# Linear attention and two expert layers in one kernel: the state's scaling on ScalarE, one mask operation for two score halves, weight splits and the last routing batch moved

## The chip, the cores and the metric

The kernel runs on 1 core of a Trainium2 chip. The metric is device time in microseconds. Engines: TensorE (PE; PEld is its weight load), VectorE (DVE), ScalarE (ACT), GpSimd (POOL) and SyncE (SP), which issues most transfers. A line number is that of the kernel before, unless the text says otherwise.

## What is computed

```python
for t in range(S):                       # attention, per batch and head; D = 48, S = 768
    state = alpha[:, :, t, :, None] * state + np.einsum('bhd,bhe->bhde', k[:, :, t], v[:, :, t])
    y[:, :, t] = np.einsum('bhd,bhde->bhe', q[:, :, t], state)
...
logits = xn @ en.T / tau                 # rows of x and of the 8 experts' embeddings, normalized
expert_idx = np.argmax(logits, axis=1)   # each of 3072 tokens goes to one expert
...
    out[mask] = gate_w[mask, None] * (np.maximum(x[mask] @ w1[e], 0.0) @ w2[e])
...
h = np.maximum(np.maximum(x @ w1, x @ w2), x @ w3)   # last layer, for all tokens
return (h @ w_out).astype(np.float32)
```

## The kernel before

The 3072 tokens are 24 groups of 128: 4 sequences of 6. Eight heads are four pairs, and a pair's two heads lie on partitions 0 to 47 and 64 to 111. In a group the recurrence is done by products: VectorE makes the decay's running products from both sides (`undo`, L274, and `decay`, L287, two scans of 516 columns), keys and queries are weighed by them (L294 on VectorE, L289 on GpSimd), and the state that passes from group to group (`sbar`) is the sum of the group's own product and the state before (L382), scaled per row and pair by the next group's decay (L384).

Attention is software-pipelined in one written order, which is also the order on each engine's queue. Iteration g of the loop issues on TensorE: `sv(g)` (masked scores times values, tile xT, L339), `kback(g+1)` (keys transposed, kb, L329), `scores(g+1)` (sc, L314), `by_token(g-1)` (output turned to tokens, with the experts' logits, xp, L357), `qs(g)` (queries times state, added to xT, L347) and `update(g)` (st, L378). The first group of a sequence has no qs product, the last no kback and no update. On VectorE stand: the scans of group g+2, the mask of g+1 (`causal`, L321, one operation for each half of the pairs, each half in a bank of PSUM), keys of g+2, logits of g-1 (L365), L382 and L384. ScalarE copies kb, xp and xT out of PSUM, squares xp (jx) and runs a range check over both running products (jk, L298). GpSimd weighs queries and scatters tokens' rows to their expert's place in memory (L469).

Routing runs in batches of groups (`SIZES`); a batch's steps on VectorE, with one ranking product on TensorE (rk, L407 to L410), are spread over the iterations by `slot("P")` to `slot("E")` and a string of letters. `fetch_first` reads the first 224 rows of the first expert back (xa) once 18 groups are scattered.

Weights of the experts come in units of 128 hidden columns. A unit is split into two float32r parts by `split_w(u)`: two casts on ScalarE (L218, L219), then, a step later, one subtraction on GpSimd (L221) and one on VectorE (L222). Units 0 to 4 are split during the last iterations, cast behind iteration 19 + u and subtracted behind sv of the next.

After the loop: `turn_first` (three pairs of transposes of xa, tile ta, L461), by_token and logits of the last group, routing of the last batch, the first products of the expert with the 224 rows (`up`, tile h, L561 to L563; `down`, tile y, L589 to L591), the last scatters, and `fetch(0)`, which reads the first expert's other rows (xb) when all scatters have landed; their transposes are L505. Then come the other experts and the last layer.

Of the kernel before, what the change touches and what calls it, by code (L numbers as in the profile page):

```python
# [9 lines left out]
F32 = mybir.dt.float32  # L10
# [12 lines left out]
C = 128  # L23
# [17 lines left out]
LOADS = (14, 16, 21, 23)  # L41
SPLITS = (19, 20, 21, 22, 23)
# [6 lines left out]
SIZES = (4, 4, 4, 4, 2, 2, 2, 2)  # L49
# [11 lines left out]
def fused_kernel(ctx, tc, qT, kT, aT, vn, emb, tau, w1, w2, m1, m2, m3, mo,  # L61
# [24 lines left out]
    ps_s = pctx.enter_context(tc.tile_pool(name="ps_s", bufs=2, space=PSUM))  # L86
    ps_sc = pctx.enter_context(tc.tile_pool(name="ps_sc", bufs=3, space=PSUM))
# [219 lines left out]
    def scores(g):  # L307

        t = cur[g]
        t["sc"] = [ps_sc.tile([128, NP, C], F32, tag="sc", name=f"sc_{g}_{j}") for j in range(2)]  # L310
        for p in range(NP):
            for j in range(2):
                c = slice(p * C, (p + 1) * C)
                nc.tensor.matmul(t["sc"][j][:, p], t["kh"][own(j), c], t["qh"][own(j), c], start=(p == 0),  # L314
                                 stop=(p == NP - 1), skip_group_check=True)

    def causal(g):
        t = cur[g]
        t["ss"] = [wk.tile([128, NP, C], F32, tag="ss", name=f"ss_{g}_{j}", bufs=4) for j in range(2)]
        for j in range(2):  # L320
            nc.vector.tensor_mul(t["ss"][j], t["sc"][j], mask.unsqueeze(1).broadcast_to([128, NP, C]))  # L321
# [12 lines left out]
    def sv(g):  # L334
        t = cur[g]
        t["xT"] = ps_x.tile([128, NP, C], F32, tag="xp", name=f"xT_{g}")[0:HR]
        for p in range(NP):
            for j in range(2):
                nc.tensor.matmul(t["xT"][lanes(j), p], t["v"][:, p, lanes(j)], t["ss"][j][:, p],  # L339
                                 start=(p == 0), stop=(p == NP - 1 and g % NCH == 0), skip_group_check=True)  # L340
# [30 lines left out]
    def update(g):  # L371
        if g % NCH == NCH - 1:
            return
        t = cur[g]
        st = ps_s.tile([128, 512], F32, tag="sr", name=f"st_{g}")[0:HR, 0:NP * D].rearrange("p (a d) -> p a d", d=D)
        for p in range(NP):
            for j in range(2):
                nc.tensor.matmul(st[lanes(j), p], t["kn"][:, p, lanes(j)], t["v"][:, p, own(j)],  # L378
                                 start=(p == 0), stop=(p == NP - 1), skip_group_check=True)
        cur[g + 1]["sbar"] = nxt = wk.tile([HR, NP, D], F32, tag="sbar", name=f"sbar_{g}")  # L380
        if g % NCH > 0:
            nc.vector.tensor_add(nxt, st, t["sbar"])  # L382
            st = nxt
        nc.vector.tensor_mul(nxt, st, by_pair(cur[g + 1]["PR"][:, 1])[:, :, 0:1].broadcast_to([HR, NP, D]))  # L384
# [71 lines left out]
    def turn_first():  # L456
        xa = exp[0]["xa"]
        for k in range(KD):
            tp = ps_sc.tile([128, 2, 2, C], F32, tag="sc", name=f"ta_{k}").rearrange("p i j t -> p (i j t)")[:, 0:AW]
# [93 lines left out]
    def up(u, c):  # L553
        i = u // NF1
        a, t, w = wtiles[u][0], exp[i], c.stop - c.start
        if "h" not in pools:
            hp = ps_sc.tile([128, 2, 2, C], F32, tag="sc", name=f"h_{u}_{c.start}").rearrange("p i j t -> p (i j t)")[:, 0:w]
# [7 lines left out]
        def act():  # L565
            if "e" not in pools:
                hs = wk.tile([128, 2, AW], F32R, tag="ss", name=f"hs_{u}", bufs=4)
# [38 lines left out]
    with tc.manual_schedule():  # L606
# [29 lines left out]
        splits = iter(())  # L636
        for g in range(NT):
# [9 lines left out]
            step(splits)  # L647
# [34 lines left out]
            if g in SPLITS:  # L682
                splits = split_w(SPLITS.index(g))
                step(splits)
        turn_first()
        by_token(NT - 1)
        logits(NT - 1)
        chain = route(len(SIZES) - 1)
# [9 lines left out]
        step(splits)  # L698
        keep(exp[0]["xa"], meta[0:AW], "ids_a")
        up(*order[2])()  # L700
    pctx.close()
# [129 lines left out]
    with tc.manual_schedule():  # L831
        gate_steps = gates()
        conv = convert(todo)
        for s, (u, c) in enumerate(order + [(NU, None)]):
# [11 lines left out]
            if len(SPLITS) <= u + LEAD < NU:  # L846
# [283 lines left out]
```

## Time and profile before

| | |
|---|---|
| median of 3 runs | 697.91 us (696.7 to 698.08) |
| the profiled execution | 696.05 us, span 694.3 us |
| PE busy | 674.1 us (97%) |
| DVE, ACT, POOL busy | 414.7, 262.2, 290.4 us |
| attention and routing | to some 145 us of the span |

Times in rows count from the span's start. A group in an L row is all instructions of a line; in a timeline row, those that follow each other. "[1.69 <-DVE ss L321]" says that the engine was idle for 1.69 us before it and that VectorE's L321, writing ss, ended that. Matmuls are pipelined: the start of the next piece tells more than a piece's own duration. A float32 product is recorded as two matmuls.

### The profile page before, as it was taken

The page shows a single profiled execution, that of the slowest core. Times are in us where ns is not written, and L with a number is a line of the kernel's source. Part 1 is how long each engine was busy: PE and PEld are TensorE (multiplying, and loading weights), DVE is VectorE, ACT ScalarE, POOL GpSimd, SP SyncE. Part 2 cuts the span into 40 slices and gives each one's busy share as a digit, 9 for nine tenths or more (in the row PEclk, how much of TensorE's full clock was granted, in tenths as well). Part 3 has the DMA queues.
Part 4 walks back from the last instruction along what each step waited for, and adds up shares of the span by engine and source line. Part 5 has one row for each costly group of instructions (what it writes and reads, how often), then busy time and mean ns, then how long its engine had stood idle before and what let it go on. Part 6 is the DMA issues. An engine that isn't in the chain of part 4 may idle for free. (4 is left out here: it accounts for less than half of the span.)

```text
span 694.3 us, 12339 instructions
## 1 busy us (share of the span) xinstructions
PE 674.1 (97%) x4659; PEld 601.6 (87%) x4659; DVE 414.7 (60%) x770; ACT 262.2 (38%) x571; POOL 290.4 (42%) x307
## 2 busy tenths in 40 slices
PE   9999999799999999999999999999999999999994
PEld 5888887688989999999999988898898898888994
DVE  8999999863697887989987796311302203103110
ACT  4556556442545455454554322212222122212221
POOL 3325754631345455455464467224234233233331
PEclk9999999889999999999999999999999999999998
DMA  9999991153554556555741320000000000000000
GB/s 242 269 241 231 283 254 76 47 169 98 169 143 149 182 168 197 162 155 169 212 142 45 71 70 12 12 24 24 1 24 24 0 24 24 0 35 11 12 35 26
DMA packets 30818, 73.44 MB, mean 106 GB/s; under 512 B 8985, under 2 KB 10785, under 8 KB 30753
## 3 DMA queue, kind: packets, MB, share of 16 engines
q1 hardware_dynamic: 26880, 63.11, 32.6%
q0 software_dynamic: 3840, 9.48, 4.0%
q8 instruction: 38, 0.62, 0.4%
q14 instruction: 28, 0.22, 0.1%
q10 hardware_dynamic: 32, 0.01, 0.0%
HBM read 60.68 MB, written 11.90 MB: 105 GB/s over the span
## 5 line engine op out<-in xcount | busy, mean ns | idle before, releaser
L908 DVE TENSOR_TENSOR t<-p,t 128x512 f32<-128x512 f32 (+1 forms) x84 | 51.6, 614 | 189.8 <-PE p L904 187.1
L902 PE MATMUL p<-bxh,m 128*128 128x512 f32 (+1 forms) x378 | 137.1, 363 | 0.8 <-ACT t L906 0.8
L903 PE MATMUL p<-bxh,m 128*128 128x512 f32 (+1 forms) x378 | 137.0, 362 | 0.0
L904 PE MATMUL p<-bxl,m 128*128 128x512 f32 (+1 forms) x378 | 137.0, 362 | 0.0
L221 POOL TENSOR_TENSOR w<-r,w 128x384 fp32r<-128x384 f32 x64 | 71.5, 1118 | 79.7 <-ACT w L218 77.6
L915 POOL TENSOR_TENSOR fl<-t,fh 128x512 fp32r<-128x512 f32 (+1 forms) x36 | 43.4, 1207 | 139.7 <-ACT fh L914 104.4
L902 PEld LDWEIGHTS p<-bxh,m 128*128 128x128 f32 x378 | 71.1, 188 | 12.9 <-ACT t L906 1.0
L904 PEld LDWEIGHTS p<-bxl,m 128*128 128x128 f32 x378 | 71.1, 188 | 12.3
L903 PEld LDWEIGHTS p<-bxh,m 128*128 128x128 f32 x378 | 71.1, 188 | 12.0
L914 ACT CAST fh<-t 128x512 fp32r<-128x512 f32 (+1 forms) x42 | 23.5, 560 | 150.7 <-DVE t L908 150.7
L561 PE MATMUL h<-xh,w 128*128 128x224 f32 (+8 forms) x207 | 72.8, 351 | 0.4 <-DVE xl L438 0.4
L562 PE MATMUL h<-xh,w 128*128 128x224 f32 (+8 forms) x207 | 71.0, 343 | 0.8 <-POOL w L221 0.8
L563 PE MATMUL h<-xl,w 128*128 128x224 f32 (+8 forms) x207 | 70.5, 341 | 0.0
L222 DVE TENSOR_TENSOR w<-r,w 128x384 fp32r<-128x384 f32 x64 | 61.1, 955 | 13.4 <-ACT w L219 13.3
L591 PE MATMUL y<-hl,w 128*128 128x464 f32 (+8 forms) x192 | 66.3, 345 | 0.0
L589 PE MATMUL y<-hh,w 128*128 128x464 f32 (+8 forms) x192 | 65.8, 343 | 0.0
L590 PE MATMUL y<-hh,w 128*128 128x464 f32 (+8 forms) x192 | 65.7, 342 | 0.0
L571 ACT ACTIVATE hh<-h 128x464 fp32r<-128x464 f32 (+8 forms) x64 | 32.0, 501 | 63.1 <-PE h L563 63.1
L289 POOL TENSOR_TENSOR qt<-qt,PR 112x512 f32<-112x512 f32 x23 | 27.5, 1198 | 63.1 <-DVE PR L287 28.8
L572 DVE SCALAR_TENSOR_TENSOR hl<-h,hh 128x464 fp32r<-128x464 f32 (+8 forms) x64 | 36.3, 567 | 24.1 <-ACT hh L571 23.9
L923 PE MATMUL o<-wo,fh 128*128 128x384 f32 x144 | 48.4, 336 | 0.0
L924 PE MATMUL o<-wo,fh 128*128 128x384 f32 x144 | 48.4, 336 | 0.0
(204 smaller groups left out, 1356.0 us busy)
## 6 DMA issues: line engine op xcount, KB each, us to landing
r<-in_w SPq DMA_DIRECT2D x64, 384.0 KB
cr_in_m<-in_m SPq DMA_DIRECT2D x18, 384.0 KB
vt<-in_vn SPq DMA_DIRECT2D x11, 448.0 KB
exr<-xs_scratch SPq DMA_DIRECT2D x5, 675.5 KB
at<-in_aT SPq DMA_DIRECT2D x16, 193.7 KB
kt<-in_kT SPq DMA_DIRECT2D x16, 192.0 KB
qt<-in_qT SPq DMA_DIRECT2D x16, 192.0 KB
xs_scratch<-zt SPq DMA_DIRECT2D x8, 289.5 KB
```

What stands on the lines that cost most here:

```text
L221: nc.gpsimd.tensor_sub(a[:, 1], r1[:, k], a[:, 0].bitcast(F32))
L222: nc.vector.tensor_sub(b[:, 1], r2[:, k], b[:, 0].bitcast(F32))
L561: nc.tensor.matmul(hp, a[:, 0, k], t["xh"][:, k, c], start=(k == 0), stop=False)
L562: nc.tensor.matmul(hp, a[:, 1, k], t["xh"][:, k, c], start=False, stop=False)
L563: nc.tensor.matmul(hp, a[:, 0, k], t["xl"][:, k, c], start=False, stop=(k == KD - 1))
L589: nc.tensor.matmul(y, w[:, 0, sl], hh, start=(f == 0 and c.start == 0), stop=False, skip_group_check=True)
L590: nc.tensor.matmul(y, w[:, 1, sl], hh, start=False, stop=False, skip_group_check=True)
L591: nc.tensor.matmul(y, w[:, 0, sl], hl, start=False, stop=(f == NF1 - 1), skip_group_check=True)
L902: nc.tensor.matmul(pt, m[:, 0, k], xh[:, k], start=(k == 0), stop=False)
L903: nc.tensor.matmul(pt, m[:, 1, k], xh[:, k], start=False, stop=False)
L904: nc.tensor.matmul(pt, m[:, 0, k], xl[:, k], start=False, stop=(k == KD - 1))
L908: nc.vector.tensor_tensor(t0, pt, t0, op=ALU.max)
```

## The change

1. `update`: the sum L382 stays on VectorE; the scaling is done by ScalarE, in four operations of 48 columns, one per pair, with the scale read from a column of the running products. In the first group of a sequence, which has no sum, they read st in PSUM.
2. Both halves of the scores lie in one tile of two banks (`ps_sc`, one buffer of two banks instead of three of one), and one VectorE operation of 1024 columns masks them. The bank that is left goes to the pool `ps_s`, where kb, st, rk and now also ta and the first h tiles take turns in three buffers.
3. The casts of units 0 and 1 stand behind iteration 21, of 2 behind 22, of 3 behind 23, unit 4 behind the third `up`; the subtractions one step later each. The third load of weights moves from iteration 21 to 22.
4. The last batch of two groups is two batches of one. Group 22's choice stands at the end of iteration 23, its ranking ahead of `turn_first`, its places and its scatter behind; group 23's at the end.

```diff
--- before.py
+++ after.py
@@ -38,15 +38,15 @@
-LOADS = (14, 16, 21, 23)
-SPLITS = (19, 20, 21, 22, 23)
+LOADS = (14, 16, 22, 23)
+SPLITS = {21: (0, 1), 22: (2,), 23: (3,)}
...
-SIZES = (4, 4, 4, 4, 2, 2, 2, 2)
+SIZES = (4, 4, 4, 4, 2, 2, 2, 1, 1)
...
-    ps_s = pctx.enter_context(tc.tile_pool(name="ps_s", bufs=2, space=PSUM))
-    ps_sc = pctx.enter_context(tc.tile_pool(name="ps_sc", bufs=3, space=PSUM))
+    ps_s = pctx.enter_context(tc.tile_pool(name="ps_s", bufs=3, space=PSUM))
+    ps_sc = pctx.enter_context(tc.tile_pool(name="ps_sc", bufs=1, space=PSUM))
...
-        t["sc"] = [ps_sc.tile([128, NP, C], F32, tag="sc", name=f"sc_{g}_{j}") for j in range(2)]
+        t["sc"] = ps_sc.tile([128, 2, NP, C], F32, tag="sc", name=f"sc_{g}")
...
-        t["ss"] = [wk.tile([128, NP, C], F32, tag="ss", name=f"ss_{g}_{j}", bufs=4) for j in range(2)]
-        for j in range(2):
-            nc.vector.tensor_mul(t["ss"][j], t["sc"][j], mask.unsqueeze(1).broadcast_to([128, NP, C]))
+        t["ss"] = wk.tile([128, 2, NP, C], F32, tag="ss", name=f"ss_{g}")
+        nc.vector.tensor_mul(t["ss"].rearrange("p j a t -> p (j a) t"), t["sc"].rearrange("p j a t -> p (j a) t"),
+                             mask.unsqueeze(1).broadcast_to([128, 2 * NP, C]))
...
-        nc.vector.tensor_mul(nxt, st, by_pair(cur[g + 1]["PR"][:, 1])[:, :, 0:1].broadcast_to([HR, NP, D]))
+        for p in range(NP):
+            nc.scalar.activation(nxt[:, p], st[:, p], AF.Copy, scale=by_pair(cur[g + 1]["PR"][:, 1])[:, p, 0:1])
...
-            tp = ps_sc.tile([128, 2, 2, C], F32, tag="sc", name=f"ta_{k}").rearrange("p i j t -> p (i j t)")[:, 0:AW]
+            tp = ps_s.tile([128, 512], F32, tag="sr", name=f"ta_{k}")[:, 0:AW]
...
-            hp = ps_sc.tile([128, 2, 2, C], F32, tag="sc", name=f"h_{u}_{c.start}").rearrange("p i j t -> p (i j t)")[:, 0:w]
+            hp = ps_s.tile([128, 512], F32, tag="sr", name=f"h_{u}_{c.start}")[:, 0:w]
...
-        splits = iter(())
+        splits = []
+
+        def split_steps():
+            for x in splits:
+                step(x)
+            splits.clear()
+
...
             sv(g)
             slot("P")
-            step(splits)
+            split_steps()
...
-            if g in SPLITS:
-                splits = split_w(SPLITS.index(g))
-                step(splits)
+            for u in SPLITS.get(g, ()):
+                splits.append(split_w(u))
+                step(splits[-1])
+        slot("Q")
         turn_first()
+        slot("E")
         by_token(NT - 1)
         logits(NT - 1)
+        while ready:
+            scatter(*ready.pop(0))
+        split_steps()
         chain = route(len(SIZES) - 1)
...
-        step(splits)
         keep(exp[0]["xa"], meta[0:AW], "ids_a")
         up(*order[2])()
+        for _ in split_w(4):
+            pass
```

VectorE from one state to the next, in a group inside the first sequence; before:

```order
L382 TENSOR_TENSOR sbar_562<-st_553,sbar_490 112x192
L384 TENSOR_TENSOR sbar_562<-sbar_562,PR_431 112x192
L274 SCALAR_TENSOR_TENSOR PR_583<-at_94,last 112x516
L281 RECIPROCAL first_124<-PR_583 112x4
L287 SCALAR_TENSOR_TENSOR PR_583<-at_94,first_124 112x516
L321 TENSOR_TENSOR ss_0_600<-sc_0_590,mask 128x512
L321 TENSOR_TENSOR ss_1_601<-sc_1_591,mask 128x512
L294 TENSOR_TENSOR kt_98<-kt_98,PR_583 112x512
L365 TENSOR_REDUCE rawl<-xp_604 128x8
L382 TENSOR_TENSOR sbar_635<-st_626,sbar_562 112x192
```

and now (line numbers of the changed kernel, where L320 is the mask):

```order
L382 TENSOR_TENSOR sbar_557<-st_548,sbar_485 112x192
L274 SCALAR_TENSOR_TENSOR PR_581<-at_94,last 112x516
L281 RECIPROCAL first_124<-PR_581 112x4
L287 SCALAR_TENSOR_TENSOR PR_581<-at_94,first_124 112x516
L320 TENSOR_TENSOR ss_597<-sc_588,mask 128x1024
L294 TENSOR_TENSOR kt_98<-kt_98,PR_581 112x512
L365 TENSOR_REDUCE rawl<-xp_599 128x8
L382 TENSOR_TENSOR sbar_630<-st_621,sbar_557 112x192
```

L384 is gone from the queue, and one operation of 1024 columns stands for two of 512.

VectorE at the split of unit 0 (tile w_0), in iteration 20 before:

```order
L424 COPY first_rows<-oh_143 128x1
L222 TENSOR_TENSOR w_0_1825<-r_0_1428,w_0_1825 128x384
L274 SCALAR_TENSOR_TENSOR PR_1839<-at_94,last 112x516
L281 RECIPROCAL first_124<-PR_1839 112x4
L287 SCALAR_TENSOR_TENSOR PR_1839<-at_94,first_124 112x516
L321 TENSOR_TENSOR ss_0_1866<-sc_0_1856,mask 128x512
L321 TENSOR_TENSOR ss_1_1867<-sc_1_1857,mask 128x512
```

and in iteration 22 now:

```order
L382 TENSOR_TENSOR sbar_1970<-st_1961,sbar_1881 112x192
L414 TENSOR_REDUCE oh_144<-oh_143 128x8
L416 TENSOR_TENSOR fi_1888<-rk_1942,oh_143 128x16
L418 TENSOR_REDUCE sm_1887<-fi_1888 128x2
L421 CAST pos_1979<-sm_1887 128x2
L222 TENSOR_TENSOR w_0_1989<-r_0_1420,w_0_1989 128x384
L222 TENSOR_TENSOR w_1_1993<-r_0_1420,w_1_1993 128x384
L320 TENSOR_TENSOR ss_2023<-sc_2014,mask 128x1024
L365 TENSOR_REDUCE rawl<-xp_2025 128x8
L382 TENSOR_TENSOR sbar_2055<-st_2046,sbar_1970 112x192
L397 TENSOR_REDUCE sm_2061<-rawl 128x2
```

Two subtractions stand behind each other, behind the last scans and ahead of the last group's mask.

TensorE from the last group's qs (xT) to the transposes of the first expert's rows (ta) and the last by_token (xp); before:

```order
L347 MATMUL xT_2093<-qt_102,sbar_2079 48x128 x8
L461 MATMUL ta_2146<-ident,xa 128x112 x2
L461 MATMUL ta_2151<-ident,xa 128x112 x2
L461 MATMUL ta_2156<-ident,xa 128x112 x2
L357 MATMUL xp_2161<-turn_w,xt_2127 128x104 x4
```

and now:

```order
L347 MATMUL xT_2076<-qt_102,sbar_2055 48x128 x8
L408 LDWEIGHTS ones_b
L408 MATMUL rk_2136<-base_b,ones_b 128x8
L410 LDWEIGHTS ones_b
L410 MATMUL rk_2136<-oh_145,ones_b 128x8
L411 LDWEIGHTS tri
L411 MATMUL rk_2136<-oh_145,tri 128x8
L462 MATMUL ta_2140<-ident,xa 128x112 x2
L462 MATMUL ta_2145<-ident,xa 128x112 x2
L462 MATMUL ta_2150<-ident,xa 128x112 x2
L357 MATMUL xp_2160<-turn_w,xt_2110 128x104 x4
```

The ranking of group 22 (rk) stands between qs and the transposes.

## Rows read from the trace of the kernel before

**Rows 1.** Stretches: from:to, length, busy time of each engine, granted clock, DMA share, GB/s.
```profile
22.00:116.00 94.00, 92.64 (x1289) 78.01 (x1285) 92.35 (x194) 54.23 (x125) 44.06 (x49) 1.00 0.93 232
133.10:143.40 10.30, 10.30 (x83) 8.85 (x80) 5.52 (x18) 3.41 (x8) 5.68 (x8) 0.50 0.51 164
160.40:163.90 3.50, 3.50 (x20) 3.50 (x19) 0.69 (x3) 0.53 (x2) 0.00 (x0) 0.51 0.33 51
164.00:685.00 521.00, 519.85 (x2792) 474.54 (x2790) 270.72 (x445) 177.65 (x373) 215.72 (x203) 1.00 0.26 79
```
**Rows 2.** Timeline, TensorE, one group: start, duration, instruction, count, idle time before it.
```profile
21.84 1.05 PE L339 MATMUL xT<-ss,vt 128*64 128x128 f32 x15
22.82 0.60 PE L329 MATMUL kb<-ident,kt 112*128 112x112 f32 x4
23.35 1.16 PE L314 MATMUL sc<-qt,kt 48*128 48x128 f32 x16
24.44 1.14 PE L357 MATMUL xp<-turn_w,xt 112*128 112x104 f32 x8
25.51 1.08 PE L347 MATMUL xT<-qt,sbar 48*48 48x128 f32 x16
26.52 0.61 PE L378 MATMUL st<-vt,kn 128*64 128x48 f32 x15
...
27.02 1.05 PE L339 MATMUL xT<-ss,vt 128*64 128x128 f32 x15
```
**Rows 3.** Timeline, TensorE, groups 19 to 23 and the first expert's transposes.
```profile
114.17 0.17 PE L407 MATMUL rk<-base_b,ones_b 128*128 128x16 bf16 x1
...
115.86 0.41 PE L339 MATMUL xT<-ss,vt 128*64 128x128 f32 x2
...
123.56 0.43 PE L339 MATMUL xT<-ss,vt 128*64 128x128 f32 x2 [1.69 <-DVE ss L321]
...
131.75 0.43 PE L339 MATMUL xT<-ss,vt 128*64 128x128 f32 x2 [2.13 <-DVE ss L321]
...
144.86 0.80 PE L461 MATMUL ta<-ident,xa 112*128 112x112 f32 x6
```
**Rows 4.** Timeline, VectorE, one group without routing.
```profile
93.54 1.26 DVE L321 TENSOR_TENSOR ss<-sc,mask 128x512 f32<-128x512 f32 x2
...
95.90 0.36 DVE L384 TENSOR_TENSOR sbar<-sbar,PR 112x192 f32<-112x192 f32 x1
96.18 1.23 DVE L274 TENSOR_TENSOR_SCAN PR<-at,last 112x516 f32<-112x516 f32 x1
...
98.80 1.26 DVE L321 TENSOR_TENSOR ss<-sc,mask 128x512 f32<-128x512 f32 x2
```
**Rows 5.** Timeline, VectorE, beside the weight splits of units 0 and 1.
```profile
118.87 2.56 DVE L274 TENSOR_TENSOR_SCAN PR<-at,last 112x516 f32<-112x516 f32 x1
...
126.37 2.11 DVE L222 TENSOR_TENSOR w<-r,w 128x384 fp32r<-128x384 f32 x1
```
**Rows 6.** Timeline, GpSimd, the weight split of unit 0.
```profile
119.33 1.01 POOL L221 TENSOR_TENSOR w<-r,w 128x384 fp32r<-128x384 f32 x1
```
**Rows 7.** Groups by line, ScalarE: busy us, mean ns of one, idle time before.
```profile
L928 ACT ACTIVATE ot<-o,gts 128x384 f32<-128x384 f32 x24 | 13.9, 581 | 53.5 <-PE o L925 53.5
...
L360 ACT COPY xr<-xp 128x384 f32<-128x384 f32 x24 | 11.5, 480 | 44.5 <-PE xp L357 29.3 <-POOL w L221 7.8 <-POOL xr L369 4.2
```
**Rows 8.** Timeline, VectorE, last logits and routing.
```profile
144.91 0.19 DVE L365 TENSOR_REDUCE rawl<-xp 128x8 f32<-128x32 f32 x1 [1.82 <-ACT jx L362]
...
148.24 0.17 DVE L396 TENSOR_REDUCE sm<-rawl 128x2 f32<-128x16 f32 x1
...
149.28 0.18 DVE L413 TENSOR_REDUCE oh<-oh 128x8 bf16<-128x24 bf16 x1
```
**Rows 9.** Timeline, GpSimd and then TensorE: last scatter, wait for the expert's rows.
```profile
152.33 0.98 POOL L469 DMA_INDIRECT xs_scratch<-xr,pos  x1 [0.30 <-issue]
...
159.28 0.79 PE L505 MATMUL t<-ident,xb 112*128 112x112 f32 x6 [1.72 <-DMA xb<-xs_scratch]
```

More of the change, by code (lines that the diff above doesn't have):

```diff
@@ L313, in scores @@
                 c = slice(p * C, (p + 1) * C)
-                nc.tensor.matmul(t["sc"][j][:, p], t["kh"][own(j), c], t["qh"][own(j), c], start=(p == 0),
+                nc.tensor.matmul(t["sc"][:, j, p], t["kh"][own(j), c], t["qh"][own(j), c], start=(p == 0),
                                  stop=(p == NP - 1), skip_group_check=True)
@@ L338, in sv @@
             for j in range(2):
-                nc.tensor.matmul(t["xT"][lanes(j), p], t["v"][:, p, lanes(j)], t["ss"][j][:, p],
+                nc.tensor.matmul(t["xT"][lanes(j), p], t["v"][:, p, lanes(j)], t["ss"][:, j, p],
                                  start=(p == 0), stop=(p == NP - 1 and g % NCH == 0), skip_group_check=True)
@@ L566, in act @@
             if "e" not in pools:
-                hs = wk.tile([128, 2, AW], F32R, tag="ss", name=f"hs_{u}", bufs=4)
+                hs = wk.tile([128, 2, AW], F32R, tag="hs", name=f"hs_{u}", bufs=4)
                 hh, hl = hs[:, 0], hs[:, 1]
@@ L845, in fused_kernel @@
                 read_m(*todo[0][:2])
-            if len(SPLITS) <= u + LEAD < NU:
+            if NA <= u + LEAD < NU:
                 for _ in split_w(u + LEAD):
```

## The prediction

> **What bounds the kernel now.** I read the views in this order: the stretches, TensorE's order in one group, its late places, then VectorE, GpSimd and ScalarE there. In the stretches [rows 1] the experts and the last layer, 164 to 685 us, keep TensorE busy for 519.85 of 521 us: nothing that the change touches is waited for there, so what the change gains or loses before 164 us reaches the end one to one. Before that, VectorE is busy for 92.35 of the 94 us from 22 to 116, and TensorE for 92.64: two engines look full. Which of them sets the pace is read from single groups. In a group in which TensorE waits for nothing [rows 2] its six pieces start at 21.84 (sv), 22.82 (kb), 23.35 (sc), 24.44 (xp), 25.51 (qs), 26.52 (st) and 27.02 (next sv): 0.98 + 0.53 + 1.09 + 1.07 + 1.01 + 0.50 = 5.18 us. VectorE in a group without routing goes from mask to mask in 98.80 - 93.54 = 5.26 us [rows 4], and routing comes on top. So VectorE is the slower one by a little, and TensorE only just behind it.
>
> What TensorE loses to it: from sv of group 2 (21.84) to sv of group 20 (115.86 [rows 3]) are 18 groups in 94.0 us. Their floor is 18 x 5.18 = 93.2; three groups lack kb, three st (a sequence's last state isn't wanted) and three qs (a sequence's first group), 3 x 2.04 = 6.1 less; five rankings of some 0.17 us [rows 3] are 0.9 more: 88.0. So 6.0 us are waits for masks. Worse are the two groups behind: sv waits 1.69 and 2.13 us for its masks at 123.56 and 131.75 [rows 3]. There VectorE lost time to GpSimd: the scan at 118.87 took 2.56 us where one takes 1.23 [rows 4], and the weight subtraction at 126.37 took 2.11 us, while GpSimd ran its own weight subtraction from 119.33 to 120.34 in the first case [rows 5, 6]. After the second wait the clock falls: from 133.1 to 143.4 TensorE has 0.50 of it, which is 1.2 GHz instead of 2.4, and again from 160.4 to 163.9 [rows 1], behind a wait of 1.72 us for the last rows of the first expert [rows 9].
>
> **The change, part by part.** (A) *State scaled by ScalarE, one mask operation.* Each group's VectorE work loses L384, 0.36 us, of which 96.18 - 95.90 = 0.28 count, since the next scan starts under its tail, and about 0.1 of the wait for L382's result in front of it [rows 4]. The two masks take 1.26 us as a pair; from the 0.36 us of 192 columns to 1.26 of twice 512 a column is worth about 1 ns, so one operation of 1024 is 1.15 to 1.26: 0 to 0.1 less, I take 0.06. 5.26 - 0.28 - 0.1 - 0.06 = 4.8 us, below TensorE's 5.18, with 0.4 left for routing. TensorE becomes the bound, and no more than the 6.0 us can be had. Where the five steps of a batch's choice stand in a row they take 149.28 - 148.24 = 1.04 us [rows 8], more than a group's 0.4: I leave 0.8 us of waits. Term A: -5.2 us, between -6.0 and -3.
>
> ScalarE gets four scalings a group, queued behind its range check, and behind them stand the copies of the next group. No row shows one. The nearest are 581 ns (128x384 out of PSUM, scaled by a column) and 480 ns (the same size, unscaled) [rows 7]: at most 4 x 0.58 = 2.3 us, at least 4 x 0.10 = 0.4; with 48 columns I take 0.3 each less overlap, 1.0 us. ScalarE is busy 54.23 us over 18 groups [rows 1], 3.0 a group; 4.0 still fits in 5.18, so the scaled state is there before the next qs, 4.17 us after the last one's end. Cost 0; if that cover is gone, (B and rivals) it comes straight onto TensorE.
>
> The Trainium skill speaks against this part: its page "ScalarE: Activation LUTs", section "Rules for kernel authors", sends multiplications to VectorE; the same page's "What ACT_TABLE_LOAD costs" gives 186 ns plus 0.833 a column and 93 for a scale from memory, which would make an estimated 0.32 us each and 1.0 us for four back to back. By that rule the part would be a loss if ScalarE were as full as VectorE; the row of stretches has it at 54 of 94 us, and by either price the sum is the same.
>
> (B) *Splits behind the last scans.* From sv of group 20 to sv of group 22, 115.86 to 131.75, are 15.9 us; the floor is 2 x 5.18 + 0.17 = 10.5 [rows 2, 3]. The subtractions of units 0 and 1 leave these groups on both engines, and with them the scan that took 1.33 us too long and the 2.11 us. What stays are the routing steps of the batches of two: I leave 0.5 us. Term B: -4.9, between -5.4 and -3.5.
>
> The Trainium skill's page "SBUF — State Buffer", section "SBUF: two separate sides", says that GpSimd and a VectorE operation with two inputs in SBUF exclude each other for a whole instruction. The scan at 118.87 agrees: 2.56 us, over just when GpSimd's 1.01 us and a scan's 1.23 are both through. By it the two pairs of subtractions that now follow each other in group 22 can hold each other up; that is one bound in the next term.
>
> (C) *Groups 22 and 23.* From sv of 22 (131.75) to the first transposes (144.86) are 13.1 us [rows 3]; at full clock the pieces are 0.98 + 1.09 + 1.07 + 1.01 + 0.50 + 0.98 + 1.07 + 0.17 + 1.01 = 7.9. The rest, 5.2, is the half clock, and with waits like the 2.13 us gone I expect none here. New is that both pairs of subtractions, each behind its casts on ScalarE, stand ahead of the mask of group 23 on VectorE; sv of 23 waits for that. TensorE has 1.09 + 1.07 + 1.01 + 0.50 us of other work; casts of four tiles (0.48 each by the nearest row [rows 7]) after the scalings, then two subtractions of 0.5 to 2.11 and a mask of 1.2 come 0 to 2.4 us later than that. I take 1.4. Term C: -3.8, between -5.2 and -2.8.
>
> (D) *The last batch in two.* Before, the first transposes stand right behind qs of 23. Now the ranking of group 22 stands between. It needs that group's logits, which VectorE starts at 144.91, after ScalarE's pass over the same tile [rows 8], then four steps of the batch before and five of its own at 0.21 each: 144.91 + 0.1 + 1.9 = 146.9, so TensorE waits 2.0 us from 144.86. The transposes take turns in three buffers, and the third waits for a copy and a subtraction of the first (0.48 and 0.36 by the nearest rows [rows 4, 7], part of it beside the first two): 0.5. In the chain from the last logits to the rows of the first expert a weight subtraction of 384 columns now stands ahead of the last choice: 0.6. What goes is one scatter of the last two, 0.30 + 0.98 = 1.3 [rows 9]. The chain gets 2.0 + 0.5 + 0.6 - 1.3 = 1.8 us longer, and TensorE's own work in it starts 2.5 later, so the 1.72 us wait for the first expert's rows shrinks to about 0.5. Term D: +1.8, between 0 and +4.
>
> (E) *Clock.* The fall at 160.4 should go with that wait: half of 3.5 us [rows 1], -1.7. One like it is likely behind the 1.4 and 2.0 us of new waits: +1.7, between 0 and +5.1, which a fall as long as the one at 133.1 costs. Term E: 0.
>
> Sum: -5.2 - 4.9 - 3.8 + 1.8 + 0 = -12.1 us. The profiled execution took 696.05 us (span 694.3): 684. The median of the runs is 697.91, 1.86 above it, so a median of 685.8 is the forecast. DMA is left out on purpose: the inputs are asked for three pairs of groups ahead, no engine waits for one between 22 and 116 us.
>
> **Rivals.** (1) *The clock stays low at the end of attention.* The new waits of 1.4 and 2.0 us lie within some 6 us, and before a wait of 2.13 was enough for 10.3 us at 1.2 GHz. Against: behind them soon come the dense products of the expert, and behind the 1.72 us wait those were slow for 3.5 us only. It gives back 3.4 to 5 us: 690. Chance 0.17. (2) *TensorE's order has waits of its own*, so that a faster VectorE buys little in the regular groups: the state's sum still needs st of the same group, and the mask needs the scores. For it: both engines are full today. Against: a group of 5.18 exists in the trace with no wait in it. Then A is -2: 689; chance 0.08. (3) *Slower: ScalarE's queue becomes the bound.* The scalings stand behind the range check and ahead of everything of the next group. With 3.0 us a group there today the point is 2.2 us for four scalings; above it each 0.1 us costs 16 x 0.1. At 0.8 each, 3.2 us, sixteen groups lose 1.0 each, in place of A's -5.2, and the splits' casts queue behind: +5.2 + 16 + 1 of C: 708; it is slower than before from about 2.9 us on. Against: 581 ns is the row for eight times the columns. Chance 0.04; that it eats only A, 692: 0.04. (4) *Masks in one operation over two banks don't go as one*, so the part does nothing: A loses 18 x 0.06, 1 us, which is inside the range. (5) *No new wait in C, no fall of the clock*: 681; chance 0.11.
>
> **Numbers.** Forecast 0.56 (own range 682.5 to 689), and the rivals as given. The range of 8 in 10 takes the forecast, most of (1), (2) and (5): 681.5 to 692. Within 0.2% (1.4 us, about what a measurement of this kernel can tell from no change): 0.03. Slower: 0.04. Faster: 0.93.
>
> **What would show it.** A: sv's pieces follow st at once in regular groups, TensorE's period is 5.18, VectorE has gaps ahead of its sum L382, and the four scalings take some 0.3 us each. B: no scan of over 1.3 us, no wait over 0.6 us at sv of 21 and 22. C: clock at 2.4 GHz from group 20 to 23 and a wait of 0 to 2.4 us at sv of 23. D: TensorE waits some 2 us for the choice of group 22 ahead of the transposes, and under 1 us for the first expert's rows. Wrong it would be if qs waits for ScalarE in regular groups, if the clock falls for 10 us, or if the time from the first transposes to the expert's rows grows by over 4 us.

## The result and the profile after

Faster by 0.9%: 691.01 us median of six runs (690.09 to 693.95), against 698.0 for the kernel before beside it; ratio 0.9909 [0.9891, 0.9928], so about 6.4 us. Timed again later it took 692.33, ratio 0.9924 [0.9900, 0.9949]. Forecast were 685.8 and -12.1 us. The sign holds and about half of the size; 691.01 lies outside the forecast's own range (682.5 to 689) and just inside the range of 8 in 10 (681.5 to 692), the later median just outside it. The profiled execution took 690.82 us (span 689.1), 5.2 less than that of before (694.3).

Where those 5.2 us are is read at five marks in TensorE's timeline: the first product of sv of groups 2, 20 and 22, the first transposes ta, and the first transposes t of the expert's rows. (For sv of 2 that is 21.73 in before; [rows 2] begin with the row of the other fifteen products.)

| stretch, us | before | after | change | forecast |
|---|---|---|---|---|
| start to sv 2 | 21.7 | 22.15 | +0.4 | 0 |
| sv 2 to sv 20 (A) | 94.1 | 91.85 | -2.3 | -5.2 |
| sv 20 to sv 22 (B) | 15.9 | 11.3 | -4.6 | -4.9 |
| sv 22 to ta | 13.1 | 14.4 | +1.3 | -0.1 (C -3.8, 2.0 of D and 1.7 of E lie here) |
| ta to t | 14.4 | 15.8 | +1.4 | -0.2 (rest of D) |
| t to the end | 535.0 | 533.6 | -1.4 | -1.7 (E's first half) |

The start's 0.4 isn't the change's: split_only (below), which alters nothing there, has sv of 2 at 22.1 as well.

TensorE's timeline of the changed kernel from sv of 22 on (start, duration, instruction, idle time before it and what ended it); it answers to [rows 3] and [rows 9].

```profile
125.31 1.09 PE L339 MATMUL xT<-ss,vt 128*64 128x128 f32 x16 [0.30 <-DVE ss L320]
...
132.89 1.97 PE L339 MATMUL xT<-ss,vt 128*64 128x128 f32 x16 [2.73 <-DVE ss L320]
134.79 2.04 PE L357 MATMUL xp<-turn_w,xt 112*128 112x104 f32 x8
...
139.59 0.17 PE L411 MATMUL rk<-oh,tri 128*128 128x8 bf16 x1 [0.64 <-DVE oh L405]
139.69 0.98 PE L462 MATMUL ta<-ident,xa 112*128 112x112 f32 x4
...
155.51 0.79 PE L506 MATMUL t<-ident,xb 112*128 112x112 f32 x6 [0.27 <-DMA xb<-xs_scratch]
```

The waits of 1.69 and 2.13 us at sv of 21 and 22 are gone, one of 2.73 stands at sv of 23, and from it on a piece takes twice its time (sv 1.97, 1.09 at 125.31). The wait for the first expert's rows is 0.27 us where it was 1.72. The stretches, as in [rows 1] (the sixth column is ScalarE's, the granted clock stands ahead of the last two):

```profile
22.25:114.00 91.75, 89.29 (x1293) 76.50 (x1290) 88.85 (x162) 66.92 (x185) 44.92 (x49) 1.00 0.93 238
132.66:146.31 13.65, 12.29 (x76) 11.04 (x77) 7.15 (x28) 6.55 (x19) 5.42 (x6) 0.50 0.36 125
155.50:680.00 524.50, 523.04 (x2818) 477.59 (x2818) 271.18 (x448) 179.11 (x378) 216.46 (x204) 1.00 0.26 79
```

The fall at 160.4 is gone, and the fall ahead of ta is longer, 13.65 us in place of 10.24. What held up sv of 23 stands on VectorE and GpSimd (ScalarE's casts first):

```profile
126.42 1.01 ACT L385 ACTIVATE sbar<-sbar,PR 112x48 f32<-112x48 f32 x4 [0.32 <-DVE sbar L382]
127.33 0.49 ACT L218 CAST w<-r 128x384 fp32r<-128x384 f32 x1
127.73 0.51 ACT L219 CAST w<-r 128x384 fp32r<-128x384 f32 x1
...
128.27 3.43 DVE L222 TENSOR_TENSOR w<-r,w 128x384 fp32r<-128x384 f32 x2 [1.31 <-ACT w L219]
131.62 1.21 DVE L320 TENSOR_TENSOR ss<-sc,mask 128x1024 f32<-128x1024 f32 x1
...
144.67 1.77 DVE L222 TENSOR_TENSOR w<-r,w 128x384 fp32r<-128x384 f32 x1
...
128.84 1.97 POOL L221 TENSOR_TENSOR w<-r,w 128x384 fp32r<-128x384 f32 x2
```

The casts come behind the four scalings, VectorE stands idle for them for 1.31 us, and then its two subtractions take 3.43 us, with GpSimd's two in their midst. That of unit 3, ahead of the last choice, takes 1.77 us (0.6 forecast). In the steady part the mask is on TensorE's path (VectorE, then TensorE):

```profile
94.16 0.36 DVE L382 TENSOR_TENSOR sbar<-st,sbar 112x192 f32<-112x192 f32 x1 [0.85 <-PE st L378]
...
97.11 1.20 DVE L320 TENSOR_TENSOR ss<-sc,mask 128x1024 f32<-128x1024 f32 x1
...
98.36 1.09 PE L339 MATMUL xT<-ss,vt 128*64 128x128 f32 x16 [0.30 <-DVE ss L320]
99.38 0.60 PE L329 MATMUL kb<-ident,kt 112*128 112x112 f32 x4
```

VectorE waits for TensorE's state, and then TensorE for the end of VectorE's mask. Over all of this part VectorE is nearly as full as before: busy for 88.85 of 91.75 us, where it was 92.35 of 94.00 [rows 1].

### The profile page after: what moved, and what is told of

It is laid out like the page before. It is cut to its first block, busy times and chain, and to the rows that moved or that the text cites. A ratio compares the mean times of both kernels' runs of the same rounds, so it can differ in the third digit from the quotient of the medians.

```text
span 689.1 us, 12376 instructions
## 1 busy us (share of the span) xinstructions
PE 668.0 (97%) x4661; PEld 598.6 (87%) x4661; DVE 410.8 (60%) x735; ACT 279.5 (41%) x651; POOL 293.2 (43%) x307
## 5 line engine op out<-in xcount | busy, mean ns | idle before, releaser
L221 POOL TENSOR_TENSOR w<-r,w 128x384 fp32r<-128x384 f32 x64 | 71.5, 1121 | 77.9 <-ACT w L218 74.8
L222 DVE TENSOR_TENSOR w<-r,w 128x384 fp32r<-128x384 f32 x64 | 64.6, 1011 | 16.1 <-ACT w L219 16.0
L289 POOL TENSOR_TENSOR qt<-qt,PR 112x512 f32<-112x512 f32 x23 | 27.5, 1197 | 56.3 <-DVE PR L287 28.8
L573 DVE SCALAR_TENSOR_TENSOR hl<-h,hh 128x464 fp32r<-128x464 f32 (+8 forms) x64 | 36.3, 567 | 22.1 <-ACT hh L572 21.9
```

The costliest lines, as they stand in the source:

```text
L221: nc.gpsimd.tensor_sub(a[:, 1], r1[:, k], a[:, 0].bitcast(F32))
L222: nc.vector.tensor_sub(b[:, 1], r2[:, k], b[:, 0].bitcast(F32))
```

## The experiments

One table first, at the marks above, from each profiled execution; falls are those of the clock before 165 us (start, length).

| kernel | sv 2-20 | 20-22 | sv 22-ta | ta-t | falls | ratio to before |
|---|---|---|---|---|---|---|
| before | 94.1 | 15.9 | 13.1 | 14.4 | 133.1 10.2; 160.4 3.4 | 1 |
| after | 91.85 | 11.3 | 14.4 | 15.8 | 132.7 13.7 | 0.9909 [0.9891, 0.9928] |
| after_again | 91.96 | 11.3 | 12.6 | 15.5 | 138.3 6.8 | 0.9924 [0.9900, 0.9949] |
| scale_only | 92.95 | 18.0 | 9.3 | 18.9 | 122.3 13.7; 146.2 6.8 | 0.9970 [0.9940, 1.0000] |
| mask_only | 95.2 | 15.9 | 11.3 | 14.7 | 134.3 6.8 | 1.0005 [0.9981, 1.0028] |
| split_only | 95.2 | 12.1 | 10.1 | 16.4 | 139.1 6.8 | 0.9858 [0.9828, 0.9889] |
| route_undone | 95.2 | 11.3 | 10.7 | 15.9 | 97.0 6.8 | 0.9874 [0.9845, 0.9903] |
| mask_halves | 89.3 | 11.3 | 14.7 | 16.0 | 11.0 3.4; 130.5 13.7 | 0.9890 [0.9847, 0.9932] |
| fill_gap | 92.8 | 11.3 | 12.6 | 16.8 | 139.1 6.8 | 0.9887 [0.9854, 0.9920] |
| subs_three | 91.1 | 11.3 | 11.4 | 15.6 | 136.6 6.8 | 0.9852 [0.9817, 0.9888] |
| pool_next | 91.1 | 11.3 | 11.4 | 15.4 | 138.3 3.4 | 0.9858 [0.9828, 0.9888] |
| best3 | 89.3 | 11.3 | 12.3 | 16.5 | 133.2 6.8 | 0.9886 [0.9850, 0.9923] |
| best4 | 90.5 | 11.3 | 9.95 | 15.3 | none | 0.9834 [0.9803, 0.9864] |

Each stretch is from one execution, and kernels that have the same code from sv of 2 to sv of 20 show how far it scatters. Before and split_only have 94.1 and 95.2. After, after_again, subs_three and pool_next have 91.1 to 92.0; fill_gap has 92.8, and route_undone 95.2 with a stall.

**One part alone, on the kernel before.** *scale_only* takes only this:

```
-        nc.vector.tensor_mul(nxt, st, by_pair(...)[:, :, 0:1].broadcast_to([HR, NP, D]))
+        for p in range(NP):
+            nc.scalar.activation(nxt[:, p], st[:, p], AF.Copy, scale=by_pair(...)[:, p, 0:1])
```

> The kernel before with the state scaled by ScalarE and nothing else. Prediction's term A as far as it is VectorE's work: sv of 2 to sv of 20 from 94.0 to 88.6 to 89.5 us. Rival (the 6 us of waits are not VectorE's total work but its order in a group): 91 to 92. If the scaling does it all and the mask in one piece costs, this run has the shorter stretch of the two, below the 91.75 of the whole change. Groups 20 to 23 keep the slow scan and the half clock; time 692 to 696.

695.52 us. The steady part gets 1.2 us shorter, not 5, and it holds one wait of 1.41 us for keys from memory (TensorE):

```profile
70.35 1.23 PE L314 MATMUL sc<-qt,kt 48*128 48x128 f32 x16 [1.41 <-DMA kt<-in_kT]
```

Up to there it is as fast as the whole change: from sv of 2 to sv of 11 are 45.2 us here and 45.1 in the changed kernel. So, that wait aside, the scaling alone brings about what the steady part of the whole change gained. From sv of 20 to sv of 22 it takes 18.0 us. The casts now stand behind the scalings, and VectorE waits for them (VectorE, then TensorE):

```profile
118.31 1.43 DVE L222 TENSOR_TENSOR w<-r,w 128x384 fp32r<-128x384 f32 x1 [1.26 <-ACT w L219]
...
123.00 2.54 PE L339 MATMUL xT<-ss,vt 128*64 128x128 f32 x16 [2.16 <-DVE ss L321]
```

Of the 2.1 us that these groups are longer than before, 0.3 lie ahead of sv of 21 (8.0 us in place of 7.7) and 1.8 behind it, where the clock is at half from 122.3 on.

*mask_only* takes the mask in one operation, with its buffers.

```
-        for j in range(2):
-            nc.vector.tensor_mul(t["ss"][j], t["sc"][j], mask...broadcast_to([128, NP, C]))
+        nc.vector.tensor_mul(t["ss"]..., t["sc"]..., mask...broadcast_to([128, 2 * NP, C]))
```

> The kernel before with both halves of the mask in one operation over two banks (and the buffers that this takes) and nothing else. Prediction: VectorE has 0.06 us a group less, so sv of 2 to sv of 20 is 93 to 94 us, time 697. Rival (TensorE could begin sv behind the first half before, and now waits for the whole): 94.5 to 98 us; time 698 to 702.

697.31 us, no change that can be measured. The steady part is 1.1 us longer in its trace than in before, and as long as in split_only (95.2), which keeps before's two operations. The operation does go as one, in 1.20 to 1.22 us in place of 1.26 [rows 4]; rival (4) is out. Nor does it take a head start from TensorE that it had. Before, each operation masked one head of all four pairs, not half of the pairs, and sv takes both heads of a pair in turn. So the first half let one of sv's eight products go (x2 in the trace), and the second product waited for the second half. Here are group 21 in before ([rows 3] have its first product at 123.56) and group 20 in mask_only (VectorE, then TensorE, for each):

```profile
122.84 1.26 DVE L321 TENSOR_TENSOR ss<-sc,mask 128x512 f32<-128x512 f32 x2
...
124.16 1.07 PE L339 MATMUL xT<-ss,vt 128*48 128x128 f32 x14 [0.16 <-DVE ss L321]
125.16 0.60 PE L329 MATMUL kb<-ident,kt 112*128 112x112 f32 x4
```

```profile
116.04 1.20 DVE L320 TENSOR_TENSOR ss<-sc,mask 128x1024 f32<-128x1024 f32 x1
...
117.29 1.09 PE L339 MATMUL xT<-ss,vt 128*64 128x128 f32 x16 [0.33 <-DVE ss L320]
118.31 0.60 PE L329 MATMUL kb<-ident,kt 112*128 112x112 f32 x4
```

From the mask's start to the piece behind sv are 2.32 us before and 2.27 here and in the changed kernel (97.11 to 99.38).

*split_only* takes the new places of the weight splits and their loads.

```
-LOADS = (14, 16, 21, 23)
-SPLITS = (19, 20, 21, 22, 23)
+LOADS = (14, 16, 22, 23)
+SPLITS = {21: (0, 1), 22: (2,), 23: (3,)}
...
```

> The kernel before with the weight splits (and their loads) where the change puts them and nothing else. Prediction's term B: sv of 20 to sv of 22 from 15.9 to 10.8 to 12 us; term C: a wait of 1 to 3.5 us at sv of 23 and a fall of the clock of 10 to 13.7 us there, so sv of 22 to the first transposes is 12.5 to 15. Together 692 to 694.5. Rival (term B came from VectorE being lighter by the state's scaling): sv of 20 to sv of 22 stays above 13, time 695 to 698.

688.48 us: alone, it gains more than the whole change; its interval lies below both of the changed kernel's. So the other three parts together cost some 3 to 4 us on top of it. Term B stands without the lighter VectorE (12.1 us). The long wait at sv of 23 and the early fall, both expected, do not come (VectorE, then GpSimd):

```profile
131.89 1.03 DVE L222 TENSOR_TENSOR w<-r,w 128x384 fp32r<-128x384 f32 x2
...
133.83 1.97 POOL L221 TENSOR_TENSOR w<-r,w 128x384 fp32r<-128x384 f32 x2
```

Here the casts follow the range check at once, VectorE comes to its two subtractions later and finds their data there, and GpSimd's pair starts after VectorE's is over: 1.03 us, not 3.43. That it is the scalings that make the casts late in the changed kernel is read from these orders; no run takes the scalings alone out of it.

**The steady waits.** *mask_halves* is the changed kernel with the mask in two, by pairs of heads. This is not the cut of before: the first half has both heads of two pairs and lets four of sv's eight products go.

```
+        t["ss"] = [wk.tile([128, 2, NP // 2, C], F32, tag="ss", name=f"ss_{g}_{i}", bufs=4) for i in range(2)]
+        for i in range(2):
+            nc.vector.tensor_mul(t["ss"][i], t["sc"][:, :, i * (NP // 2):(i + 1) * (NP // 2)],
+                                 mask.unsqueeze(1).unsqueeze(1).broadcast_to([128, 2, NP // 2, C]))
...
-                nc.tensor.matmul(t["xT"][lanes(j), p], t["v"][:, p, lanes(j)], t["ss"][:, j, p],
+                nc.tensor.matmul(t["xT"][lanes(j), p], t["v"][:, p, lanes(j)], t["ss"][p // 2][:, j, p % 2],
```

> The changed kernel with the mask in two operations of 512 again, but split by pairs of heads, so that the first half lets the first eight products of sv go. Theory (what is left of the waits in regular groups, 3.75 us from sv of 2 to sv of 20, is TensorE waiting for the end of one long mask): sv of 2 to sv of 20 goes from 91.75 to 89.5 to 90.5 us; time 689 to 690. Rival (VectorE's total work sets the pace; two operations cost it 0.06 us a group more): 92 to 93 us from sv of 2 to sv of 20; time 691 to 692.

The steady part goes to 89.3 us. The group shown above, in this kernel (VectorE, then TensorE):

```profile
93.02 0.34 DVE L383 TENSOR_TENSOR sbar<-st,sbar 112x192 f32<-112x192 f32 x1
...
95.90 1.26 DVE L321 TENSOR_TENSOR ss<-sc,mask 128x512 f32<-128x512 f32 x2
...
97.21 0.30 PE L340 MATMUL xT<-ss,vt 128*48 128x128 f32 x1
```

Neither engine waits for the other here. From sv of 2 to sv of 20 TensorE is busy for 89.1 of the 89.3 us and VectorE for 87.5: now TensorE is the bound. best3 and best4, which cut the mask the same way, have 89.3 and 90.5, less than any kernel with one mask. Not every group gains: where a batch's choice stands, the masks follow each other after 5.5 us in both kernels (112.75 to 118.28, and 111.60 to 117.14 here). The time, 690.45, isn't measurably below the changed kernel's: this execution lost 0.8 us to a fall at 11.0 us, and the second long fall (130.5) stayed.

**The wait at sv of 23.** *subs_three* leaves the subtractions of units 0 and 1 until those of unit 2.

```
             slot("P")
-            split_steps()
+            if g != NT - 2:
+                split_steps()
```

> The changed kernel with VectorE's and GpSimd's subtractions of units 0 and 1 one group later: on VectorE they stand behind the mask and the choice of group 23 in place of ahead of that mask. Theory (the wait of 2.9 us at sv of 23 comes from the two subtractions that took 3.43 us, and the clock falls because of that wait): the mask of 23 follows its scores at about 127.5 us, the wait is under 0.4 us, the clock keeps 2.4 GHz through groups 22 and 23 or falls only later and for a shorter time; sv(22) to first transposes 14.4 -> 8 to 10 us; time 684 to 687. Rival (the clock falls anyway, since the choices of groups 22 and 23 leave TensorE waiting too): the wait goes, 10 to 13 us at 1.2 GHz stay; time 688 to 690. Rival (the casts of the units on ScalarE are what is late): the wait at sv of 23 goes, and one of over 2 us stands at the ranking or at qs of 23; 690 to 691.

687.23 us. The wait is gone; the choices now keep TensorE waiting, and a shorter fall follows these, so it is between the first theory and its rival:

```profile
129.35 1.05 PE L339 MATMUL xT<-ss,vt 128*64 128x128 f32 x15
...
134.66 0.17 PE L410 MATMUL rk<-oh,ones_b 128*128 128x8 bf16 x1 [1.08 <-DVE oh L414]
136.01 0.17 PE L411 MATMUL rk<-oh,tri 128*128 128x8 bf16 x1 [1.18 <-DVE oh L405]
```

*pool_next* leaves VectorE's two where they are and puts GpSimd's two one group later.

```
+        nc.vector.tensor_sub(b[:, 1], r2[:, k], b[:, 0].bitcast(F32))
+        if u < 2:
+            yield
         nc.gpsimd.tensor_sub(a[:, 1], r1[:, k], a[:, 0].bitcast(F32))
-        nc.vector.tensor_sub(b[:, 1], r2[:, k], b[:, 0].bitcast(F32))
...
+            again = splits[:] if len(splits) == 2 else []
             for x in splits:
                 step(x)
-            splits.clear()
+            splits[:] = again
```

> The changed kernel with GpSimd's subtractions of units 0 and 1 one group later (with that of unit 2); VectorE's two stay where they are, ahead of the mask of group 23. Theory (VectorE's two took 3.43 us because GpSimd ran its own two in the same time): they take 1.0 to 1.3 us, the mask of 23 ends some 2 us earlier, the wait at sv of 23 is 0.3 to 0.8 us in place of 2.7; time 686.5 to 689. Rival (it is the scatters, GpSimd's DMA issue, or the two casts coming late that stretch them): they still take over 2.5 us, the wait stays over 2; time 690 to 692.

687.31 us, as the theory had it (VectorE, TensorE, GpSimd; here L221 is VectorE's subtraction and L224 GpSimd's):

```profile
128.06 0.56 DVE L221 TENSOR_TENSOR w<-r,w 128x384 fp32r<-128x384 f32 x1 [1.31 <-ACT w L219]
128.88 0.61 DVE L221 TENSOR_TENSOR w<-r,w 128x384 fp32r<-128x384 f32 x1 [0.27 <-issue]
129.42 1.21 DVE L322 TENSOR_TENSOR ss<-sc,mask 128x1024 f32<-128x1024 f32 x1
...
130.69 1.09 PE L341 MATMUL xT<-ss,vt 128*64 128x128 f32 x16 [0.74 <-DVE ss L322]
...
130.02 1.96 POOL L224 TENSOR_TENSOR w<-r,w 128x384 fp32r<-128x384 f32 x2
```

The late casts stay (1.31 us), the scatters stay, and yet the two subtractions take 0.56 and 0.61 us: it was GpSimd's pair that stretched them. Of the 2.73 us, 2.0 were this and 0.7 the casts.

**The clock.** *fill_gap* puts matmuls on zeros into the wait.

```
-        t["xT"] = ps_x.tile([128, NP, C], F32, tag="xp", name=f"xT_{g}")[0:HR]
+        full = ps_x.tile([128, NP, C], F32, tag="xp", name=f"xT_{g}")
+        if g == NT - 1:
+            warm(full.rearrange("p a t -> p (a t)"), 12)
+        t["xT"] = full[0:HR]
```

> The changed kernel with twelve matmuls on zeros (bf16, 128x512, into the buffer that sv of 23 then overwrites) ahead of sv of 23 on TensorE: they need nothing that is late and last about 2.6 us, so they lie in the wait of 2.9 us and change nothing else. Theory (the idle time itself brings the clock down): sv of 23 starts at 132.9 as before, no fall at 132.7; from sv of 23 to the first transposes 4.5 to 5.5 us in place of 6.8; if no other fall follows, the time is 687 to 688.5; if the waits for the choices bring one of 6.8 us later, 688.5 to 690. Rival (the clock falls for a reason other than this wait, or by the clock of the chip): the fall stays; 691 to 692.

690.06 us. sv of 23 comes as late as ever, the fall at that place is gone, and one comes behind the choice's wait (TensorE, then two stretches):

```profile
131.37 2.76 PE L192 MATMUL xT<-wsrc 128*128 128x512 bf16 x12
134.16 1.09 PE L342 MATMUL xT<-ss,vt 128*64 128x128 f32 x16
...
139.07 0.17 PE L414 MATMUL rk<-oh,tri 128*128 128x8 bf16 x1 [1.18 <-DVE oh L408]
```

```profile
132.70:139.00 6.30, 4.96 (x53) 3.47 (x52) 4.97 (x20) 4.22 (x13) 2.38 (x5) 1.00 0.66 214
139.10:145.90 6.80, 6.31 (x30) 5.92 (x30) 3.47 (x10) 2.35 (x7) 3.79 (x4) 0.50 0.24 88
```

*after_again* is the changed kernel, unchanged.

> The changed kernel once more, unchanged, on the chip and in the session of the other two. All theories: the ratio of the first runs, 0.991, within 0.003; the wait of 2.7 us at sv of 23 again. If the fall of the clock belongs to the wait alone, it lasts 13.7 us again and starts at 132 to 133; if it depends on more than the wait, it may be absent or start elsewhere (an execution of the kernel with the batch of two had the same wait and no fall behind it), and then the stretch from sv of 22 to the first transposes is 11 in place of 14.4 us.

692.33 us. The same wait, and no fall right behind it; one of 6.8 us comes behind the choice's wait (TensorE, then two stretches):

```profile
132.90 1.09 PE L339 MATMUL xT<-ss,vt 128*64 128x128 f32 x16 [2.72 <-DVE ss L320]
...
137.81 0.17 PE L411 MATMUL rk<-oh,tri 128*128 128x8 bf16 x1 [1.19 <-DVE oh L405]
```

```profile
132.90:138.20 5.30, 3.91 (x50) 3.32 (x51) 3.53 (x18) 4.20 (x12) 1.99 (x3) 1.00 0.60 196
138.30:145.10 6.80, 6.20 (x30) 5.92 (x28) 3.98 (x13) 2.28 (x7) 3.33 (x4) 0.50 0.26 91
```

So the wait alone does not decide the fall, and fill_gap, one execution, can't prove that filling it does. For a link speak the places: the fall starts within the wait's last us or right at its end in after (132.7), mask_halves (130.5; its wait of 2.35 us ends at 131.2) and scale_only (122.3, the wait above). In before and mask_only it starts later, 1.4 and 1.1 us behind the end of waits of 2.13 and 2.70. Over the whole run the first six executions of the changed kernel had 0.983 to 0.988 of the clock, this one 0.991. It is also the fastest of its eight; the others had 0.980 to 0.988 and took 690.0 to 695.1 us. Between the two profiled executions the early fall of 13.65 us, in place of the later one of 6.8, is worth 1.8 us from sv of 22 to ta (14.4 against 12.6) and 2.1 us of the whole (690.82 against 688.74).

**The last batch.** *route_undone*:

```
-SIZES = (4, 4, 4, 4, 2, 2, 2, 1, 1)
+SIZES = (4, 4, 4, 4, 2, 2, 2, 2)
```

> The changed kernel with the last routing batch as one of two groups again. Prediction's term D: without the choice of group 22 ahead of the first transposes they come 1 to 2 us earlier behind sv of 23; the rows of the first expert come one scatter (1.3 us) later, so that first transposes to the expert's rows grows by 2 to 3 us; time 691 to 692.5. Rival (the split of the batch costs more than the scatter it saves): 689 to 690.5.

689.78 us, on the rival's side, though its interval overlaps the changed kernel's. From ta to t it takes 15.9 us (after_again 15.5), not 2 to 3 more. Its profiled execution has a stall of its own at 95 us, with the fall at 97.0; behind the same wait at sv of 23 it has no fall at all:

```profile
135.96 1.09 PE L339 MATMUL xT<-ss,vt 128*64 128x128 f32 x16 [2.71 <-DVE ss L320]
...
139.14 0.88 PE L462 MATMUL ta<-ident,xa 112*128 112x112 f32 x6
```

From sv of 22 to t it needs 26.7 us, after_again 28.1, after 30.2. The split of the batch costs some 1.5 us here, its clock included: after_again has a fall of 6.8 us in this stretch, route_undone none.

**Together.** *best3* joins subs_three, the two half masks, and:

```
-        split_steps()
         chain = route(len(SIZES) - 1)
         for _ in range(5):
             step(chain)
+        split_steps()
```

> The changed kernel with three things moved: the subtractions of units 0 and 1 behind the mask and the choice of group 23; the mask in two halves by pairs of heads; the subtraction of unit 3 behind the choice of group 23's experts on VectorE. If the three add up: 691.0 - 3.8 (the first, measured) - 2 to 2.5 (sv of 2 to sv of 20 was 2.5 us shorter with the halves) - 1 to 1.5 (that subtraction took 1.77 us in front of the last choice) = 683 to 684.5. Rival (what the halves gain is lost at the start, where the clock fell for 3.4 us with them, and the first expert waits for something else than the last choice): 685.5 to 687.

688.85 us: the parts don't add up, and the rival's 687 is passed as well. The first expert's rows are used at 151.63, 23.9 us behind sv of 23 (22.6 in the changed kernel), and the wait for them is 1.45 us: what comes sooner ahead of them is lost there. The last scatter is issued 1.2 us sooner than in subs_three (143.94 against 145.18), but takes 4.2 us to land in place of 3.0, so the read of the rows (SyncE, xb) is issued at 148.30 in both. Loads of weights were still moving when it was issued; that they hold it up is not shown. *best4* also undoes the split of the batch.

```
-SIZES = (4, 4, 4, 4, 2, 2, 2, 1, 1)
+SIZES = (4, 4, 4, 4, 2, 2, 2, 2)
```

> The changed kernel with four things: the subtractions of units 0 and 1 behind the mask and the choice of group 23, the mask in two halves by pairs of heads, the subtraction of unit 3 behind the last choice, and the last routing batch as one of two groups. Theory (with the batch in two, the choice of group 22 stands ahead of the last turn to tokens, xp of 23, on TensorE, and so the last choice comes later than the one scatter it saves): from sv of 23 to xp of 23 8.7 to 9.3 us become about 4, the rows of the first expert come at 145 to 148 us (151.6 without this fourth part), no fall of the clock over 7 us; time 682 to 685. Rival (the rows are bound by the two scatters): they come at 151 to 153; time 687 to 689.

685.65 us (682 to 685 expected), ratio 0.9834 [0.9803, 0.9864], the lowest; it beats before and after, while its interval overlaps those of split_only, subs_three and pool_next. TensorE's timeline:

```profile
128.37 1.05 PE L340 MATMUL xT<-ss,vt 128*64 128x128 f32 x15
...
133.26 1.08 PE L463 MATMUL ta<-ident,xa 112*128 112x112 f32 x6 [0.61 <-DMA xa<-xs_scratch]
134.18 1.05 PE L358 MATMUL xp<-turn_w,xt 112*128 112x104 f32 x8
```

sv to xp of 23 is 5.9 us (9.3 in best3; expected 4, but the transposes now wait for their own rows), t comes at 148.53, 3.1 us sooner than in best3, and the clock is full from 22 to 150 us. Its lead over best3 is in the traces, where best3 also has a fall of 6.8 us that it has not; the two intervals overlap.

## Why the prediction was right in sign and half wrong in size

- **What bounds the kernel, t to the end.** Held. 533 to 535 us stand behind t in every run, so what is gained ahead of it reaches the end.
- **A, -5.2, measured -2.3.** What failed is "TensorE becomes the bound", with "I leave 0.8 us of waits". Against the forecast's floor of 88.0 us 3.9 are left, and neither engine is the bound: TensorE is busy for 89.29 and VectorE for 88.85 of 91.75 us, and each waits for the other. VectorE lost 3.5 us of busy time (92.35 to 88.85), where 18 groups of 0.28 + 0.06 would be 6.1. One reason is in the count: of these 18 groups only 15 scale a state. Another is the mask: its 1.20 us was forecast right, but the 0.06 are not gained, since the weighing of the keys behind it (L294) grew from 729 to 815 ns (means from 22 to 112 us, a single one of 1.67 us included). It starts sooner and still ends 0.55 us behind an operation of GpSimd's (last section). What then kept TensorE waiting was the end of the whole mask: halves by pairs bring the steady part to 89.3, 4.8 us less than before and nearly the forecast. This is a new gain and not the return of an old one, since the cut by heads let only one product go. Rival (2) ("A is -2", chance 0.08) has the right size; but the loop through st and the state's sum that it gives as the reason is the same in mask_halves, so that loop alone does not hold A at -2.
- **ScalarE's four scalings.** Taken as 1.0 us, measured 0.88 to 1.02 for the four, which overlap (0.32 each), and no qs of a regular group waits for them. "The splits' casts queue behind" stood in rival (3) as a small change; VectorE waits 1.26 us for a cast in scale_only and 1.31 in the changed kernel.
- **B, -4.9, measured -4.6.** Held: scans of 1.22 to 1.24 us in these groups, waits of 0.15 and 0.30 at sv of 21 and 22. split_only shows its cause.
- **C, the new wait: 1.4 taken, 2.7 came**, above the bound of 2.4. Its mechanism was named (both pairs in group 22 can hold each other up), and pool_next shows it; the size was off because the upper bound was a single subtraction's row, 2.11, and the pair took 3.43. The rest of C, that the half clock of before is saved, held where no early fall came (after_again, route_undone); the profiled execution had one of 13.65 us.
- **D, +1.8 (2.0 ahead of ta, -0.2 behind).** route_undone puts the split of the batch at some +1.5 us with its clock, so the sign held in the traces; the medians don't separate it. Behind ta 1.4 us were lost, not 0.2 gained: the subtraction of unit 3 took 1.2 us more than its 0.6, and the third transposes' wait came at half clock. best3, which moves that subtraction among other things, gained nothing there (16.5 us from ta to t). "The wait shrinks to about 0.5" doesn't follow from its own figures: 1.72 + 1.8 - 2.5 are 1.0. It was 0.27.
- **E.** The late fall is gone and the wait for the expert's rows is 0.27 us: -1.4 for -1.7. That the fall hung on that wait isn't shown: scale_only and mask_only wait 2.0 us there, five others 1.3 to 1.5, and none has a fall behind it. The new one came near its price, 1.8 to 2.1 for 1.7, but not in every execution.
- **Rival (1)** (690, chance 0.17) came close in time, and its long fall came in the profiled execution, but the clock is only 2 of the 5 us between result and forecast.
- **Rival (3)** did not come. Its 708 counts A's 5.2 twice: the 16 us are already counted from a group of 5.18, in which A is lost or won.
- **The signs named in advance.** Of those for the forecast, the clock of groups 20 to 23 and a wait of 0 to 2.4 us at sv of 23 failed, as did sv following st at once. Of the three for being wrong, one came: a fall of over 10 us.
- The sum: start 0.4, A 2.9, B 0.3, sv 22 to ta 1.4, ta to t 1.6 and the end 0.3 more than forecast are the 6.9 us between -12.1 and -5.2. Of the 1.4, 1.3 is the longer wait.

## What to carry to other kernels

How an operation is cut decides when its consumer may go: halves by heads let one product of eight start, as good as one whole operation, and halves by pairs let four. Count that, not only the busy time. When work is moved from a full engine to a free one, look at what stands behind it in the free one's queue: here four scalings of 1 us in all stand ahead of the weight casts, and VectorE's and GpSimd's subtractions met that miss each other in split_only. Try each part of a change alone: one of these four had more than the gain of all.

## What the runs showed of the hardware

VectorE's operations with two inputs in SBUF were held up by GpSimd's for whole instructions, small ones too: in best3 a comparison of 128x16 that takes 0.18 us elsewhere took 1.72 us beside GpSimd's pair (1.55 in subs_three; VectorE, then GpSimd),

```profile
128.50 1.72 DVE L400 TENSOR_TENSOR fi<-rawl,sm 128x16 f32<-128x16 f32 x1
...
128.21 1.97 POOL L221 TENSOR_TENSOR w<-r,w 128x384 fp32r<-128x384 f32 x2
```

while the mask, whose scores come from PSUM, took its usual 1.21 us beside the same pair in pool_next (129.42), and the pair its usual 1.96. The Trainium skill's page "SBUF — State Buffer", section "SBUF: two separate sides", says this of two SBUF inputs; both rows agree.

The same holds of the weighing of keys (L294) and GpSimd's of queries (L289) in each regular group. Where the first starts over 0.2 us before the second ends, it ends 0.55 us behind it, whether it takes 0.77 us (before, 99.98) or 1.67 (after, VectorE, then GpSimd):

```profile
67.01 1.67 DVE L294 TENSOR_TENSOR kt<-kt,PR 112x512 f32<-112x512 f32 x1
...
66.93 1.20 POOL L289 TENSOR_TENSOR qt<-qt,PR 112x512 f32<-112x512 f32 x1
```

So 0.06 us saved ahead of it are lost again. Which of two goes first isn't told by their starts: the scan of 2.56 us [rows 5] starts 0.46 us ahead of GpSimd's subtraction [rows 6], and it is the scan that waits.

The same wait of 2.7 us on TensorE was followed at once by 13.65 us at 1.2 GHz in one execution, by full clock for another 5 us in a second one of the same kernel, and in route_undone by no fall at all. The Trainium skill's page "TensorE: Matmul & The Clock Gate", section "Part 1: The HAM clock gate", says that the gate's monitor runs free of the program; these runs agree, but none shows it directly. What decides in a single execution stays open; half clock is to be priced as a chance, not as a certainty.
